# A recurrence and its MLP on one core: instruction order from a table instead of from priorities

## The chip, the cores and the metric

The kernel runs on one core of a Trainium2 chip. TensorE (PE) multiplies matrices, VectorE (DVE) and ScalarE (ACT) work element by element and move results out of PSUM, GpSimd (POOL) and SyncE (SP) mostly issue DMAs. Each engine runs its own instruction list in order, and the engines wait for one another through semaphores. The metric is the device time of one launch in microseconds; lower is better.

## What is computed

A recurrent layer with a matrix state for each of 4 x 8 heads runs over 768 positions, and its output goes through an MLP with the activation h tanh(softplus(h)).

```python
# B, H, S, D = 4, 8, 768, 40
state = zeros(B, H, D, D)
for t in range(S):
    y[:, :, t] = einsum('bhd,bhde->bhe', r_t, state)
    Sa = einsum('bhde,bhe->bhd', state, a_t)
    state = state * w_t[:, :, None, :] - einsum('bhd,bhe->bhde', Sa, b_t)
    state = state + einsum('bhd,bhe->bhde', v_t, k_t)
x = y.transpose(0, 2, 1, 3).reshape(B * S, H * D)     # 3072 x 320
h = x @ w_in                                          # 320 x 2048
g = h * tanh(softplus(h))
out = g @ w_out                                       # 2048 x 320
```

## The kernel before

**The recurrence in chunks.** The 768 positions are cut into 12 chunks of 64. Within a chunk the recurrence is solved with matrices, so that only one small state is passed from chunk to chunk. The work falls into preparation, which doesn't depend on the state, and steps, which do. Two chunks share one inverse; call them a pair. The letters are those that the change uses for units of work; c is a chunk, be one of two halves of its preparation, g one of two groups of heads in a step, n a pair.

- Preparation (`pre_a`, lines 126-203), for each (c, be): loads of decay and vectors (l), two scans and their products on VectorE (p, lines 145-170), a store of the decay products P to the DRAM tensor pD (line 172), the decay matrix (r, lines 162-168), eight Gram matmuls (g, lines 182-194) and transposes (k, lines 196-203).
- Inverse (`pre_inv`, lines 205-221), for each pair: i, a triangular inverse on VectorE, 60 dependent small instructions between transposes.
- After it (`post_inv`, lines 223-260): m, a corner product in two halves of 32 matmuls, with a copy by ScalarE between them (line 235); copies of blocks into bdT (b, d, lines 249-251); and a merge into KT (t, lines 255-260).
- A step (`step`, line 349), for each (c, g): the state is copied into VS (V, line 277); A multiplies it with KT (line 284), and ScalarE writes UVT (line 286); T transposes UVT (line 293); D transposes the state (line 304); B multiplies and VectorE masks (lines 314-316); C gives output and state change (lines 334-339), and VectorE builds the new state (lines 342-346). Then the output is stored to DRAM (yD), and v, u and q, the loads of the next chunk, are issued by GpSimd.

**The MLP.** x is the product of yD and pD, read back from DRAM (`load_yp`, lines 467-476) and split into two parts, xh and xl, so that products of reduced precision add up to full precision. Six blocks i of 512 rows are worked through, each in eight slices q: `mlp1` (h, line 584) makes 16 matmuls of 512 columns, ScalarE applies the activation (line 586), and the result is split (H, lines 589-590); `mlp2` (y, lines 604-606) makes 24 matmuls of 320 columns into four PSUM tiles. y runs three slices behind h. The weights come as 64-bit values and are converted and split on ScalarE and VectorE (`load_f32`, lines 445-464, and `split`, line 489): twelve conversions for w_in, eight for w_out.

**What sets the order.** The kernel is written in a program order, and a planner orders the instructions of each engine by priority and its own estimate of readiness. `at(tc, k)` (line 44) moves a part up or down by an offset from the table OFF (line 38), and ORDER and SORD set the order of the parts. The result is one fixed list for each engine; in the run nothing is reordered.

**Where the weights and the MLP stand.** The conversions of the first quarter of w_in (`early`) have priority over the start, the rest (`first`) stand with step 9, three of w_out (`second`) before step 10, and five (`third`) after the first slice of the MLP. The MLP itself is written behind the last step; its first blocks move forward among the last steps only as far as the planner moves them.

Of the kernel before, what the change touches and what calls it, by code (L numbers as in the profile page):

```python
# [36 lines left out]

OFF = {'I': 80, 'T1': 80, 'P00': -40, 'P10': 80, 'P11': 40, 'b0': 15, 'c0': 600, 'u0': -15, 'u1': 250, 'd0': 250,
       'd1': 150, 'W': 600, 'V': 400, 'E': 150, 'I0': 600, 'I1': 300, 'I2': 300, 'I3': 300, 'I4': 300, 'p4': 15,
       'I5': 300, 'J5': 600, 's0': 150, 's2': -15, 's3': 80, 's4': 250, 's6': -15, 's7': -40, 's8': 150, 's10': -150}  # L40
# [3 lines left out]
def at(tc, k):  # L44
    return tc.high_priority(offset=OFF[k]) if OFF.get(k) else nullcontext()

# [32 lines left out]
def attention(ctx, tc, I, yD, pD, nch, M):  # L79
    nc = tc.nc  # L80
# [3 lines left out]
    ps_u = pool("ps_u", NU, space=PSUM)  # L84
    ps_q = pool("ps_q", NQ, space=PSUM)
    ps_a = pool("ps_a", NA, ictx, "right", space=PSUM)
    M.early_pools(pctx)
    ps_g = pool("ps_g", NG, pctx, "right", space=PSUM)
# [18 lines left out]
    V.memset(z, 0.0)  # L107
    for w, b in zip(wab, bkb):
        V.memset(w, 1.0)
        G.memset(b, 0.0)  # L110
    for t in [d1] + [x.rearrange("p s k a t -> p (s k a t)") for x in adb[:NAD]]:
        A.copy(t, z.broadcast_to(t.shape))
    for t in bdT:
        G.memset(t, 0.0)
# [5 lines left out]
    for t in VS + [UVT] + bdr[:NBR] + ST:  # L120
        G.memset(t, 0.0)

    RW, W2, HA, BKN, GP, KT = {}, {}, {}, {}, {}, {}
    LQ, SQ, OQ, PQ = (dict(S=SP, G=G, A=A)[x] for x in QS)

    def pre_a(c, be):
        n = 2 * c + be
        wa, bk, ad = wab[n % NWA], bkb[n % NWA], adb[n % 2]
# [6 lines left out]
        if (c, be) == (0, 0):  # L135
            LQ.dma_start(out=cst, in_=I['cst'])
            for t in bkb:
                A.copy(t[:, :, 128:168], cst[:, 256:296].unsqueeze(1).broadcast_to([128, 8, 40]))
        wz, a = wa[:, 0:521], wa[:, 528:1040]
# [20 lines left out]
        if be == 1:  # L160

            RW[c] = wk.tile([128, 2, 16], F32, name="rw", bufs=4)
            pt = ps_g.tile([128, 2, 16], F32, name="pa")
            for b2 in range(2):
                for al in range(2):
                    PE.matmul(pt[b2 * 64:b2 * 64 + 64, al], ident[:, al * 64:al * 64 + 64], W2[b2].rearrange("p a b -> p (a b)"),
                              start=(al == 0), stop=True, skip_group_check=True)
            A.copy(RW[c], pt)
        bk4 = bk[:, :, 0:128].rearrange("p s (x t) -> p s x t", x=2)
        V.tensor_tensor(out=bk4, in0=bk4, in1=E3[:, :, 0:64].unsqueeze(2).broadcast_to([128, 8, 2, 64]), op=ALU.mult)  # L170
        for al in range(2):
            PQ.dma_start(out=pD[c, be, :, al], in_=P[al * 64:al * 64 + 40])

        if c % 2 == 0 and be == 0:
            GP[c // 2] = iw.tile([128, 32, 2, 32], F32, name="GP", bufs=NGP)
# [6 lines left out]
        for s0 in (0, 3, 6):  # L182
            m = min(3, 8 - s0)
            pt = ps_g.tile([128, 3, 168], F32, name="pa")
# [10 lines left out]

        bkn = wk.tile([128, 664], F32, name="bkn", bufs=NBKN)
        BKN[c, be] = bkn
        G.memset(bkn[:, 640:664], 0.0)
        for s0 in (0, 4):
            pt = ps_g.tile([128, 4, 2, 64], F32, name="pa")  # L200
# [4 lines left out]
    def pre_inv(n):  # L205
# [11 lines left out]
        TT = iw.tile([128, 32, 32], F32, name="TT", bufs=NTT)  # L217
        V.transpose(TT.rearrange("p u t -> p t u"), X)
        T1 = gp[0:64, :, 0]
        V.transpose(T1, TT[0:64])  # L220
        return TT, T1

    def post_inv(n, TT, T1):
        gp = GP[n]
        for h in range(2):
            with at(tc, 'T%d' % h):
                px = ps_a.tile([64, 16, 32], F32, name="pa")
                for j in range(16):
                    u = h * 16 + j
                    for al in range(2):  # L230
                        q = slice(64 + al * 32, 96 + al * 32)
                        PE.matmul(px[al * 32:al * 32 + 32, j], gp[q, u, 0], TT[q, u], start=(j == 0), stop=True,
                                  skip_group_check=True)
                X = iw.tile([64, 16, 32], F32, name="X2", bufs=NX2)
                A.copy(X, px)
                py = ps_a.tile([64, 16, 32], F32, name="pa")
                for j in range(16):
                    u = h * 16 + j
                    for al in range(2):
                        q = slice(al * 32, 32 + al * 32)  # L240
                        PE.matmul(py[q, j], T1[q, u], X[q, j], start=(j == 0), stop=True, skip_group_check=True)
                for be in range(2):
                    c = 2 * n + h
                    bd = bdT[be]
                    us = slice(h * 16 + be * 8, h * 16 + be * 8 + 8)
                    for al in range(2):
                        q0 = slice(al * 32, al * 32 + 32)
                        q1 = slice(64 + al * 32, 96 + al * 32)
                        A.copy(bd[q0, :, al, 0:32], TT[q0, us])  # L249
                        A.copy(bd[q1, :, al, 32:64], TT[q1, us])  # L250
                        A.copy(bd[q0, :, al, 32:64], py[q0, be * 8:be * 8 + 8])  # L251
# [407 lines left out]
```

## Time and profile before

| | us |
|---|---|
| median of 3 runs | 830.3 |
| lowest and highest run | 823.98 and 833.24 |
| span of the profiled execution, first to last instruction | 821.8 |
| TensorE busy in that span | 722.7 |
| VectorE busy | 458.7 |
| ScalarE busy | 428.7 |

The profile gives the span of the profiled execution; a time of its own beside that isn't shown, so 830.3 is set against 821.8, and 8.5 us lie between the median and the span. In a row of stages stand, after the limits and the length, the busy time and the count of instructions of TensorE's matmuls (PE), its weight loads (PEld), VectorE, ScalarE and GpSimd, then the granted TensorE clock as a share of full speed, the busy share of the DMA engines and GB/s. In a row of groups stand line, engine, operation, tiles written and read, shapes and count, then the busy time in us and the mean of one in ns, then the engine's idle time just before and what ended it. In a row of waits stand the waiting engine and line, what it waited for, the sum in us, the count, and the longest. A row of the chain has start, length and what ran. An fp32 matmul that isn't a transpose has two records in the trace; the table of the change counts it once.

### The profile page before, as it was taken

To read this page: it belongs to the slowest core of one execution; us is meant where nothing else is said; L and a number is where in the kernel's file an instruction comes from. 1 tells how busy PE (TensorE), PEld (TensorE's weight loads), DVE (VectorE), ACT (ScalarE), POOL (GpSimd) and SP (SyncE) were. 2 spreads that over 40 slices of the span, in tenths; PEclk is the share of its full clock that TensorE was granted. 3 is DMA by queue.
4 is the path that set the end of the run, shared out by engine and by line. 5 is a ranking of instruction groups with operands and counts; after the bars stand their busy time and mean duration, and the time that the engine had idled before them with its cause. 6 is when DMAs were issued, how large, how long until landed. Compare 5 with 4: busy or idle time off the path is not lost.

```text
span 821.8 us, 17217 instructions
## 1 busy us (share of the span) xinstructions
PE 722.7 (88%) x7048; PEld 644.8 (78%) x7048; DVE 458.7 (56%) x957; ACT 428.7 (52%) x931; POOL 103.4 (13%) x182
## 2 busy tenths in 40 slices
PE   2635798899889889888786899999999999999997
PEld 2524697788778778788676789999999999999997
DVE  6689878749899757988954558311312212111110
ACT  5533556784586867567685555343333333432331
POOL 8100012123223022221102100000000000000000
PEclk9855679999999999999999999999999999999999
DMA  6522224323433134423528755210300100000000
GB/s 169 143 65 81 57 53 96 99 67 97 118 103 76 59 96 105 83 58 111 142 76 207 160 157 135 59 51 1 77 33 0 55 17 1 33 1 1 33 1 32
DMA packets 58206, 61.81 MB, mean 75 GB/s; under 512 B 25536, under 2 KB 48704, under 8 KB 58128
## 3 DMA queue, kind: packets, MB, share of 16 engines
q1 hardware_dynamic: 49296, 40.94, 18.3%
q0 software_dynamic: 8832, 19.79, 10.0%
q8 instruction: 55, 0.90, 0.5%
q14 instruction: 23, 0.19, 0.1%
HBM read 48.79 MB, written 11.86 MB: 74 GB/s over the span
## 4 chain that ended last, share of the span: by engine, by line
PE 52%; ACT 9%; DVE 7%; DMA 3%; issue 2%; SPq 0%; ACTq 0%; DVEq 0%
PE ph L584 21%; PE po L605 7%; PE po L604 7%; PE po L606 7%; PE pa L258 2%; PE pa L186 2%; DMA xp<-pD 1%; DVE tmp L214 1%; DVE XL L216 1%; PE pq L314 1%; ACT bdT L249 1%; PE pu L284 1%; ACT bdT L250 1%; DMA cv_d<-in_wi 1%; ACT KT L260 1%
## 5 line engine op out<-in xcount | busy, mean ns | idle before, releaser
L590 DVE TENSOR_TENSOR gl<-g,gh 128x1024 fp32r<-128x1024 f32 x48 | 58.6, 1224 | 207.5 <-ACT gh L589 207.5
L586 ACT ACTIVATE g<-ph 128x512 f32<-128x512 f32 x96 | 57.3, 598 | 180.5 <-PE ph L584 180.3
L186 PE MATMUL pa<-bk,ad 128*128 128x168 f32 x384 | 85.6, 376 | 42.8 <-DVE bk L170 15.0
L604 PE MATMUL po<-w_oh,gh 128*128 128x320 f32 x384 | 118.3, 308 | 0.0
L605 PE MATMUL po<-w_ol,gh 128*128 128x320 f32 x384 | 118.3, 308 | 0.0
L606 PE MATMUL po<-w_oh,gl 128*128 128x320 f32 x384 | 118.3, 308 | 0.0
L584 PE MATMUL ph<-xh,w_ih 128*128 128x512 f32 x288 | 112.7, 393 | 2.0 <-ACT xh L568 2.0
L186 PEld LDWEIGHTS pa<-bk,ad 128*128 128x128 f32 x384 | 71.5, 235 | 48.2 <-issue 22.8
L584 PE MATMUL ph<-xh,w_il 128*128 128x512 f32 x288 | 97.1, 391 | 0.0
L584 PE MATMUL ph<-xl,w_ih 128*128 128x512 f32 x192 | 75.1, 391 | 0.0
L605 PEld LDWEIGHTS po<-w_ol,gh 128*128 128x128 f32 x384 | 72.1, 188 | 2.2
L604 PEld LDWEIGHTS po<-w_oh,gh 128*128 128x128 f32 x384 | 72.1, 188 | 1.8
L606 PEld LDWEIGHTS po<-w_oh,gl 128*128 128x128 f32 x384 | 72.1, 188 | 0.0
L584 PEld LDWEIGHTS ph<-xh,w_ih 128*128 128x128 f32 x288 | 54.1, 188 | 12.1 <-ACT xh L568 2.2
L584 PEld LDWEIGHTS ph<-xh,w_il 128*128 128x128 f32 x288 | 54.0, 188 | 11.6 <-issue 0.2
L216 DVE TENSOR_TENSOR XL<-XL,tmp 128x30 f32<-128x30 f32 (+9 forms) x180 | 58.7, 326 | 2.4
L214 DVE TENSOR_TENSOR tmp<-XL 128x30 f32<-128x30 f32 (+9 forms) x180 | 58.2, 324 | 2.3
L258 PE MATMUL pa<-bdT,HA 128*104 128x128 f32 x384 | 52.2, 289 | 7.0 <-ACT bdT L251 5.5
L258 PEld LDWEIGHTS pa<-bdT,HA 128*104 128x104 f32 x384 | 46.7, 179 | 11.1 <-ACT bdT L251 7.2
L314 PE MATMUL pq<-bdr,UVT 128*128 128x128 f32 x384 | 53.4, 284 | 0.4 <-ACT UVT L286 0.3
L334 PE MATMUL pq<-UVQ,bkn 128*64 128x104 f32 (+1 forms) x768 | 44.7, 254 | 7.8 <-DVE UVQ L316 5.5
L589 ACT CAST gh<-g 128x1024 fp32r<-128x1024 f32 x48 | 50.1, 1048 | 1.3
(89 smaller groups left out, 1212.6 us busy)
## 6 DMA issues: line engine op xcount, KB each, us to landing
wa<-in_wa SPq DMA_DIRECT2D x48, 162.5 KB
bk<-in_bk SPq DMA_DIRECT2D x48, 160.0 KB
cv_d<-in_wi SPq DMA_DIRECT2D x12, 512.0 KB
cv_d<-in_wo SPq DMA_DIRECT2D x8, 640.0 KB
pD<-P POOLq DMA_DIRECT2D x48, 81.2 KB, 2.2
VS<-in_vN POOLq DMA_DIRECT2D x24, 160.0 KB, 3.4
UVT<-in_vD POOLq DMA_DIRECT2D x24, 160.0 KB, 3.9
bdr<-in_rD POOLq DMA_DIRECT2D x24, 160.0 KB, 4.4
```

Source lines behind the costliest of these rows:

```text
L186: PE.matmul(pt[:, j], ad[:, s0 + j].rearrange("p k a t -> p (k a t)"), bk[:, s0 + j], start=(j == 0), stop=True, skip_group_check=True)
L214: V.tensor_tensor(out=tv, in0=X[:, i + 1:32, i:i + 1].broadcast_to([128, 31 - i, i]), in1=X[:, i:i + 1, 0:i].broadcast_to([128, 31 - i, i] ...
L216: V.tensor_tensor(out=X[:, i + 1:32, 0:i], in0=X[:, i + 1:32, 0:i], in1=tv, op=ALU.add)
L258: PE.matmul(pk[:, j], ha[:, s0 + j], bd[:, s0 + j].rearrange("p a t -> p (a t)"), start=(j == 0), stop=True, skip_group_check=True)
L314: PE.matmul(pq[:, s], UVT[:, g * 4 + s, be * 128:be * 128 + 128], br[:, be, g * 4 + s].rearrange("p a t -> p (a t)"), start=(s == 0), stop ...
L584: PE.matmul(ph, w, x, start=(n == 0), stop=(n == 7), skip_group_check=True)
L586: A.activation(g[:, j], ph, AF.Mish)
L589: A.copy(gh, g)
L590: V.tensor_tensor(out=gl, in0=g, in1=gh.bitcast(F32), op=ALU.subtract)
L604: PE.matmul(po[k], gh[:, j, t], oh, start=(f == 0), stop=False, skip_group_check=True)
L605: PE.matmul(po[k], gh[:, j, t], ol, start=False, stop=False, skip_group_check=True)
L606: PE.matmul(po[k], gl[:, j, t], oh, start=False, stop=(f == 15), skip_group_check=True)
```

## The change

Five things change; the arithmetic of the outputs stays.

1. The priorities go. Every part becomes a named unit (`U['A3.1']` is step A of chunk 3, group 1), `sequence()` writes the units in a program order, and `Lanes.order()` walks a table, PLAN, that lists for each of the five engines which unit's next instruction comes next. Consecutive instructions are joined by dependencies that carry order alone.
2. In the program order the load and split of x0, the last quarter of w_in (w3) and the first four slices h0.0 to h0.3 stand ahead of step 10, so ahead of the last two steps. In PLAN h0.0 follows D11.1.
3. Of w_in's first quarter only the loads and one conversion up to its last VectorE instruction stay at the start. The rest, and w1, w2 and w3, follow the inverse i5. All of w_out is converted in the MLP, in halves of 320 columns, with two load buffers (`CVA = 2`), in place, without the tile cv_m.
4. PSUM is four pools of two banks for the whole kernel; the h tiles alternate between those of Gram and inverse, the y tiles take those of the steps. g has two buffers for three; gh and gl keep six.
5. pD is stored in runs of 64 elements without the gap of one, and x is loaded with 12 DMAs for a block in place of 16, the decay in runs of 256 elements where it had 64.

```diff
-def at(tc, k):
-    return tc.high_priority(offset=OFF[k]) if OFF.get(k) else nullcontext()
+class Lanes:
+    def order(self):
+        queues = {}
+        for i in self.tc.nc.cur_bb.bb.instructions:
+            if self.of.get(i.name, '/')[0] not in '/+':
+                queues.setdefault(str(i.engine).split('.')[-1], {}).setdefault(self.of[i.name], []).append(i)
+        info = mybir.DependencyInfo(mybir.DependencyClass.NoSync, mybir.DependencyReason.DATA)
+        for e, plan in PLAN.items():
+            last, q = None, {k: iter(v) for k, v in queues[e].items()}
+            for t in plan.split():
+                k, n = (t.split('*') + ['1'])[:2]
+                for _ in range(int(n)):
+                    i = next(q[k])
+                    if last is not None:
+                        self.tc.add_manual_dep(i, last.name, info, reason='plan')
+                    last = i
+            assert all(next(x, None) is None for x in q.values())
...
+    for n in range(nds):
+        if n == nds - 1:
+            s.extend(('/i', '+i', 'x0', 'X0', 'w3'))
+            s.extend('%s0.%d' % (k, q) for q in range(NEA) for k in ('hH' if q < NGA else 'h'))
+        step(2 * n)
+        if n + 2 < nds:
+            pre(n + 2)
+        if n + 1 < nds:
+            inv(n + 1)
+        if n + 2 == nds:
+            s.extend(('/p', '+p', 'w0', 'w1', 'w2'))
+        step(2 * n + 1)
...
-            PQ.dma_start(out=pD[c, be, :, al], in_=P[al * 64:al * 64 + 40])
+            PQ.dma_start(out=pD[c, be, :, al].rearrange("e (s t) -> e s t", t=64), in_=P3[al * 64:al * 64 + 40, :, 0:64])
...
-                ph = ps_h.tile([128, T], F32, name="ph")
+                ph = (ps_g, ps_a)[nph[0] % 2].tile([128, T], F32, name="pa")
+                nph[0] += 1
...
+                for x, d in ((y, yD), (p, pD)):
+                    src = d[2 * i + c].rearrange("b e a (g t) -> (b e a g) t", g=2)
+                    SP.dma_start(out=x[:, 0:2, t], in_=src[0:256].rearrange("(k p) t -> p k t", k=2))
+                    for k in range(2):
+                        SP.dma_start(out=x[k * 64:k * 64 + 64, 2, t], in_=src[256:320])
```

Parts of PLAN, for TensorE the first merge and step, pair 1, and the end of the steps; for VectorE the start and steps 9 to 11; for SyncE the start and the MLP's first loads. `m1.0*32` means the next 32 matmuls of unit m1.0.

```
PE:  g3.1*6 m0.0*32 g3.1*2 k3.1*4 m0.0*32 k3.1*4 t0.0*4 g4.0*3 t0.0*4 g4.0*3 t0.1*8 A0.0*16 A0.1*16
...
     m1.0*32 r5*4 g5.1*3 m1.0*32 g5.1*5 t2.0*4 k5.1*4 t2.0*4 t2.1*4 k5.1*4 t2.1*4 m1.1*32
     A2.0*16 m1.1*32 A2.1*16 t3.0*4 B2.0*4 T2.0*8 B2.0*4 T2.1*8
...
     m2.0*32 r7*4 g7.1*3 m2.0*32 g7.1*5 t4.0*4
...
     A6.0*16 A6.1*16 T6.0*4 m3.1*32 B6.0*8 t7.0*4 g10.0*3 B6.1*8 T6.0*4 T6.1*4 t7.0*4 T6.1*4 D6.0*4 g10.0*5 C6.0*12 D6.1*4
...
     g11.1*6 m4.0*32 g11.1*2 m4.0*32 k11.1*4 t8.0*8 t8.1*8 m4.1*32 A8.0*16 m4.1*32 B8.0*8
...
     m5.1*32 A10.0*16 m5.1*32 A10.1*16 t11.0*8 T10.0*8 t11.1*4 T10.1*4 t11.1*4 B10.0*8 T10.1*4 D10.0*4
     B10.1*8 D10.1*4 C10.0*24 C10.1*24 A11.0*16 A11.1*16 D11.0*4 D11.1*4 h0.0*8 h0.1*8 h0.2*8 h0.0*8
     B11.0*8 h0.3*8 B11.1*8 h0.1*8 C11.0*24 h0.2*8 C11.1*24 h0.4*8 h0.3*8 h0.5*8 h0.4*8 h0.5*8 h0.6*8
     h0.7*8 h0.6*8 h0.7*8 h1.0*8 y0.0*12
DVE: z*3 w0*3 p0.0*6 p0.1 p0.0 p0.1 p0.0 p0.1*4 g0.0 p0.1 g0.0 p0.1 g0.0*2 g0.1 p1.0*6 g0.1*2 p1.1 g0.1 p1.0
...
     i5*7 C9.0 C9.1 w0*4 B9.0*2 B9.1 w0*2 B9.1 w0 C9.0 w0 C9.0*2 w0 C10.0 w1*3 C9.1*3 C10.1 w1*6 B10.0 w1
     B10.0 w1 B10.1*2 w1 w2 C10.0 w2*2 C10.0*2 w2 C10.1*3 X0*3 w2*8 B11.0*2 H0.0 B11.1 w3 B11.1 w3*3 H0.1
SP:  w0*2 l0.0*2 l0.1*2 l0.0*3 l0.1*2 w0 l1.0*2
...
     w1*3 w2 x0*12 w2*2 x1*4 w3 x1*7 w3 x1 w3 W0*2
```

More of the change, by code (lines that the diff above doesn't have):

```diff
@@ new lines, in blocks, with lower @@
+    def blocks(c, be):
+        n, bd = c // 2, bdT[be]
+        us = slice(c % 2 * 16 + be * 8, c % 2 * 16 + be * 8 + 8)
+        for al in range(2):
+            q0 = slice(al * 32, al * 32 + 32)
+            q1 = slice(64 + al * 32, 96 + al * 32)
+            A.copy(bd[q0, :, al, 0:32], TT[n][q0, us])
+            A.copy(bd[q1, :, al, 32:64], TT[n][q1, us])
+    def lower(c, be):
+        for al in range(2):
+            q0 = slice(al * 32, al * 32 + 32)
+            A.copy(bdT[be][q0, :, al, 32:64], PY[c // 2, c % 2][q0, be * 8:be * 8 + 8])
@@ new lines, in merge @@
+    def merge(c, be):
+        kt = wk.tile([104, 8, 128], F32, name="KT", bufs=NKT)
+        KT[c, be] = kt
+        ha = HA[c, be]
+        for s0 in (0, 4):
+            pk = ps_a.tile([128, 512], F32, name="pa")[0:104].rearrange("p (s t) -> p s t", s=4)
+            for j in range(4):
+                PE.matmul(pk[:, j], ha[:, s0 + j], bdT[be][:, s0 + j].rearrange("p a t -> p (a t)"), start=(j == 0), stop=True,
+                          skip_group_check=True)
+            A.copy(kt[:, s0:s0 + 4], pk)
@@ L414, with store @@
[L414 to L425 removed]
+    def store(c):
+        for be in range(2):
+            OQ.dma_start(out=yD[c, be], in_=YEV[c][be * 64:be * 64 + 40].rearrange("p a s t -> p a (s t)"))
+    for c in range(nch):
+        for be in range(2):
+            for k, f in dict(l=ld, p=scan, g=gram, k=natural, b=blocks, d=lower, t=merge).items():
+                U['%s%d.%d' % (k, c, be)] = partial(f, c, be)
+        U['r%d' % c] = partial(decay, c)
+        for g in range(2):
+            for k, f in dict(V=state, A=step_a, B=step_b, T=step_u, D=step_d, C=step_c).items():
+                U['%s%d.%d' % (k, c, g)] = partial(f, c, g)
+        for k, f in dict(v=load_vs, u=load_uv, q=load_r, o=store).items():
+            U['%s%d' % (k, c)] = partial(f, c)
@@ L426 @@
+    for n in range(nch // 2):
+        U['i%d' % n] = partial(inverse, n)
+        for h in range(2):
+            U['m%d.%d' % (n, h)] = partial(corner, n, h)
+    U['/p'] = pctx.close
+    U['/i'] = ictx.close
+I32 = mybir.dt.int32
+NQ1 = 3
+NEA = 4
+CVA = 2
 NX = 2
 NXP = 1
-NHB = 3
-NGB = 6
+NHB = 2
+NGA = 2
+NGB = 4
+NOS = 2
 LAG = 3
@@ L545, in third, with w_in @@
-    def third(self):
-        wp = self.pool("w2c", 1)
-        with self.tc.tile_pool(name="cvc", bufs=CVC, side="right") as cv:
-            self.w_out(wp, cv, range(NO1, 8))
-    def run(self, nsc):
+    def w_in(self, wp, cv, q):
+        h = wp.tile([128, 3, 512], F32R, name=f"w_ih{q}")
+        l = wp.tile([128, 3, 512], F32R, name=f"w_il{q}")
+        self.ih[q], self.il[q] = h, l
+        for k in range(3):
+            self.split(cv, h[:, k], l[:, k], self.I['wi'][:, (q * 3 + k) * 512:(q * 3 + k) * 512 + 512])
@@ L615, in run @@
+        U['+p'], U['+i'], U['+e'] = first, second, third
+        for q in range(4):
+            U['w%d' % q] = partial(w_in, q)
+        for q in range(8):
+            U['W%d' % q] = partial(w_out, q)
         for i in range(nsc // 2):
+            U['x%d' % i] = partial(load_x, i)
+            U['X%d' % i] = partial(split_x, i)
             for q in range(8):
-                wait.append((i, q) + mlp1(q, *x))
-                if (i, q) == (0, 0):
-                    self.third()
-                if q == 3 and i + 1 < nsc // 2:
-                    nx = load_x(i + 1)
```

589 lines of the change are left out of this document (323 added, 266 removed).

## The prediction, made before the changed kernel ran

> **What bounds the kernel now.** I read the page's span first, then busy time by stage, then the waits of TensorE, then those of VectorE at the start. The stages are cut where the chain changes: the first state matmul (A0, line 284) starts at 109.8 us, step 10 at 434.8, and from 480 the MLP runs alone.
>
> ```profile
> span 821.8 us, 17217 instructions
> core 0: us, PE busy (x) PEld busy (x) DVE busy (x) ACT busy (x) POOL busy (x), PEclk, DMA share, GB/s
> 0.00:50.00 50.00, 24.48 (x111) 21.00 (x112) 34.49 (x68) 25.48 (x65) 19.54 (x36) 0.86 0.53 141
> 50.00:100.00 50.00, 26.70 (x142) 22.07 (x142) 46.39 (x117) 19.75 (x58) 5.07 (x10) 0.62 0.24 70
> 100.00:109.80 9.80, 9.02 (x134) 8.23 (x128) 9.55 (x25) 6.24 (x15) 1.02 (x2) 0.50 0.35 86
> 109.80:434.80 325.00, 289.10 (x4337) 256.02 (x4338) 255.40 (x632) 226.61 (x574) 68.50 (x120) 0.98 0.34 90
> 434.80:480.00 45.20, 36.51 (x455) 30.72 (x452) 26.11 (x39) 23.60 (x43) 8.52 (x13) 0.96 0.79 168
> 480.00:816.00 336.00, 336.00 (x1883) 306.11 (x1882) 86.80 (x80) 125.73 (x176) 0.75 (x2) 1.00 0.14 39
> ```
>
> From 480 to 816 TensorE is never idle: no order can shorten that part unless work is taken out, and none is. Before it TensorE idles 49 us in the first 100, 325.0 - 289.1 = 35.9 us in the middle and 45.2 - 36.5 = 8.7 us in steps 10 and 11. In the start VectorE is the bound: 46.4 of 50 us busy between 50 and 100, and its inverse i0 must end before m0.0 can start. All that a new order can win lies in these stages.
>
> **The change part by part, by stage.**
>
> *Start (to A0.0).* The old order puts three whole conversions of w_in (lines 461-463, 495) into VectorE's first 50 us; the table keeps three instructions of one (w0*3) and sends the rest behind i5.
>
> ```profile
> L463 DVE SCALAR_TENSOR_TENSOR cv_w<-cv_d,cv_w 128x512 int32<-128x512 int32 x3 | 2.1, 691 | 0.1
> L462 DVE SCALAR_TENSOR_TENSOR cv_w<-cv_m,cv_w 128x512 int32<-128x512 int32 x3 | 2.1, 689 | 0.1
> L495 DVE SCALAR_TENSOR_TENSOR w_il<-cv_w,w_ih 128x512 fp32r<-128x512 f32 x3 | 2.0, 677 | 0.0
> L461 DVE TENSOR_SCALAR cv_w<-cv_m 128x512 int32<-128x512 int32 x3 | 1.3, 439 | 3.0 <-ACT cv_m L459 2.8
> 7.15 0.69 DVE L463 SCALAR_TENSOR_TENSOR cv_w<-cv_d,cv_w 128x512 int32<-128x512 int32 x1
> DVE HA L191 <- ACT HA L190: 6.6, 7, 2.2
> DVE wa L157 <- ACT ad L155: 3.8, 3, 1.6
> DVE GP L193 <- ACT GP L189: 0.4, 1, 0.4
> cv_d<-in_wi SPq DMA_DIRECT2D x12, 512.0 KB
> ```
>
> The three cost 2.1 + 2.1 + 2.0 + 1.3 = 7.5 us; what stays is 0.44 + 0.69 + 0.69 = 1.8; so 5.7 us leave VectorE ahead of i0. The waits of VectorE between 7.5 and 50 us sum to 10.8. The table puts instructions of the next scan into them (p0.1 between the last ones of p0.0, p1.1 between those of p1.0), where the old order mostly stands still. Between 0 and 10.8 I take half, 5.4, since the filler itself waits for loads. Against it: SyncE now issues two 512 KB loads of w_in ahead of l0.0's data, where there was one: 0.52 MB at the 141 GB/s of that stage is 3.7 us, or nothing if the loads were not what VectorE waited for (it is busy with the first conversion until 7.8). I take 2.0. Start: -5.7 - 5.4 + 2.0 = -9.1 us, between -16.5 and -2.0.
>
> *Middle (A0.0 to step 10).* The same matmuls in another order; the dependencies that hold it join instructions of one engine and add none. The largest waits of TensorE, and the rows that price them:
>
> ```profile
> PE pa L258 <- ACT bdT L251: 5.5, 5, 1.5
> PE pu L293 <- ACT UVT L286: 4.9, 5, 1.9
> PE pa L241 <- ACT X L235: 4.5, 5, 2.1
> L286 ACT ACTIVATE UVT<-pu 128x512 f32<-128x512 f32 x24 | 14.4, 600 | 15.3 <-PE pu L284 15.2
> L235 ACT COPY X<-pa 64x512 f32<-64x512 f32 x12 | 6.9, 573 | 0.3 <-PE pa L232 0.2
> L251 ACT COPY bdT<-pa 32x256 f32<-32x256 f32 x48 | 17.3, 361 | 3.8 <-PE pa L241 3.0
> 312.65 1.91 PE pa L186 x12
> 247.41 0.69 PE pu L284 x16
> ```
>
> Each of the three is a round trip over ScalarE: a corner product to its copy to the merge (m, d, t), a state product to its copy to the transposes (A, T), the two halves of m. In the table nearly all of them have other matmuls between the two ends. m1.0 and t2.0 are parted by five of g5.1, which are ten records of 1.91 / 12 = 0.16 us, so 1.6 us over two copies of 0.36. A6.0 and T6.0 are parted by A6.1, 32 records or 1.4 us over a copy of 0.60. The halves of m2.0 are parted by r7 and three of g7.1. The thin ones are four of twelve halves of m, with a bare A.0 between (m1.1, m4.1, m5.1) or two of g11.1 (m4.0). I take three quarters of 14.9 us: 11.2. The other 21.0 us are many small waits on evacuations; in-order queues that drift from the table's durations will make new ones, so I take a quarter: 5.3. Middle: -16.5 us; the ends are -35.9 (no idle left) and 0 (every wait only changes place).
>
> *Steps 10 and 11.*
>
> ```profile
> PE pu L293 <- ACT UVT L286: 3.3, 2, 2.6
> PE pq L334 <- DVE UVQ L316: 3.1, 1, 3.1
> PE ph L584 <- ACT xh L568: 2.0, 1, 2.0
> 451.31 0.49 DVE L461 TENSOR_SCALAR cv_w<-cv_m 128x640 int32<-128x640 int32 x1 [3.47 <-ACT cv_m L459]
> 451.72 0.68 DVE L316 TENSOR_TENSOR UVQ<-pq,cst 128x512 f32<-128x512 f32 x1
> 452.46 0.76 PE L334 MATMUL pq<-UVQ,bkn 128*64 128x104 f32 x12 [3.15 <-DVE UVQ L316]
> ACT cv_m L459 <- DMA cv_d<-in_wo: 5.6, 1, 5.6
> ```
>
> The wait on UVT is covered: m5.1 and t11.0 now stand between A10 and T10, so 3.3 us go. x0's twelve loads fetch the decay in runs of 256 elements instead of 64, in twelve DMAs where sixteen were, and h0.0 stands after A11 and D11, not ahead of A11.1: of the 2.0 us on xh I take 1.0. The 3.1 us stay: conversions w1 and w2 stand ahead of step masks as before. The h blocks between D11 and B11 win nothing by themselves; they are the same matmuls drawn forward. -4.3 us, between -8.7 and 0.
>
> *MLP.* Each h and y pair takes a fixed time:
>
> ```profile
> 490.72 3.65 PE ph L584 x16
> 799.18 3.65 PE ph L584 x16
> L495 DVE SCALAR_TENSOR_TENSOR w_ol<-cv_w,w_oh 128x640 fp32r<-128x640 f32 x8 | 6.6, 823 | 4.8 <-ACT w_oh L494 4.7
> L172 POOL DMA_DIRECT2D pD<-P x48 | 25.0, 525 | 186.2 <-DVE w L150 72.8 <-DVE tmp L214 42.8 <-DVE P L147 40.6
> L270 POOL DMA_DIRECT2D UVT<-in_vD x24 | 18.1, 757 | 57.1 <-PE pq L314 57.1
> ```
>
> 43 steps in 308.46 us, 7.17 each. All eight w_out tiles are converted here, in halves, where three were done earlier. An instruction on a half lies between half of 823 ns and the 690 of a 512-wide one; 16 halves of four are 26 to 44 us on a VectorE that has 336 - 86.8 = 249 us free. Cost 0; the cover is lost only if W0 is late for y0.0, which ten half blocks of h (ten of 1.83 us) precede. Buffers of g (2 for 3) and gh/gl (still 6) are freed by y and split_g blocks ahead: 0. The stores of pD become runs of 64 elements: a POOL issue between 525 ns and the 757 of UVT, at most 11 us on an engine with over 250 us free in the middle: 0. The reordered loads v, u, q keep their place behind the reads that free their tiles: 0.
>
> **Sum.** -9.1 - 16.5 - 4.3 = -29.9 us: span 791.9. The median of 830.3 lies 8.5 over the profiled span, so 800.4, rounded to 800.
>
> **The rivals.**
>
> *Everything is covered.* If three quarters of every idle stage goes and the start reaches -11, it is -11 - 26.9 - 6.5 = -44.4: 786. For it speaks that all three large waits have one remedy; against it that VectorE is itself busy 255 of 325 us.
>
> ```profile
> PE pa L186 <- DVE bk L170: 15.0, 1, 15.0
> PE pa L186 <- ACT ad L155: 10.6, 1, 10.6
> PE pa L186 <- DVE HA L191: 6.8, 2, 6.3
> ```
>
> *The clock.* The granted clock is 0.62 and 0.50 in the two rows to 109.8, after waits of 15.0, 10.6 and 6.3 us, and 0.98 in the middle, where no wait is over 2.1. At full clock the 9.02 us before A0.0 would take 4.5, another -4.5: 796. The table fills VectorE's waits, not TensorE's during i0, so I don't add it; 1 in 20, inside the case above. The Trainium skill says the same ("TensorE: Matmul & The Clock Gate", Part 1): half clock after an idle window of some 3.4 us, full after as long a busy one. By that rule, as the trace agrees, the start stays slow and the sum stands.
>
> *VectorE becomes the bound.* If masks and scans stand behind inverse instructions that are drawn forward, about half of the gain is left: -15, 815.
>
> *The waits only change place.* The old order is also a fixed one, and interleaves too. Then middle and end give nothing and the start some 4: 826.
>
> *Conversions block the steps: slower.* VectorE is in order. In the rows above one conversion waits for its load and the mask of B10 behind it makes TensorE wait 3.15 us. The table has nine whole conversions (w1, w2, w3) from step 9 on, with two load buffers, and x0's and x1's loads stand in the same SyncE queue. At the 5.6 us that ScalarE waited there, nine cost 50.4, net +20.5: 851. It cancels the gain at 29.9 / 9 = 3.3 us each and is slower by over 1% from 4.2.
>
> **How the numbers follow.** One per cent, 8.3 us, is about what this measurement tells from no change. Forecast 0.50; all covered 0.12; VectorE bound 0.13; waits change place 0.13; conversions block 0.12. Faster is the first three, 0.75; same 0.13; slower 0.12. The range reaches from 784, just under the covered case, to 832, past the case of no change; the slower case is left out, with some 0.05 below. The forecast's own range is 788 to 813.
>
> **What would show it.** Right: A0.0 starts near 100 us; step 10's A near 409; the waits on bdT, UVT and X sum to under 5 us; MLP steps stay at 7.17 without idle TensorE. Wrong: VectorE conversions with idle time before them from cv_m and masks queued behind; new TensorE waits on evacuations in the middle; an idle TensorE before y0.0.

## The result, and the profile after

The new kernel takes 757.2 us (median of 4 runs, 754.1 to 760.3) where the kernel before took 828.2 beside it: ratio 0.914, 95% interval 0.908 to 0.920. A second series gave 757.7 us and 0.919 (0.915 to 0.923). So the direction was right and the size was not: 71 us were won where 30 were forecast, and 757 lies far under the range's low end of 784.

The page of the new kernel, and its busy time by stage (columns as before: the stretch, its length, then busy time of each engine, granted clock, DMA share, GB/s). The stages are cut at the same events, the first state matmul A0 at 105.5, step 10's at 367.0 and the end of the last step at 417.8:

```profile
span 754.3 us, 17264 instructions
```

```profile
0.00:50.00 50.00, 21.60 (x112) 17.34 (x112) 36.12 (x71) 24.19 (x63) 22.32 (x38) 0.91 0.58 151
50.00:100.00 50.00, 27.36 (x249) 23.32 (x250) 46.55 (x106) 22.84 (x67) 5.66 (x8) 0.67 0.23 64
100.00:105.50 5.50, 5.50 (x39) 5.36 (x37) 4.85 (x19) 3.36 (x8) 0.00 (x0) 0.79 0.36 88
105.50:367.00 261.50, 254.78 (x4221) 235.00 (x4220) 243.80 (x617) 211.72 (x550) 75.82 (x123) 1.00 0.41 100
367.00:417.80 50.80, 45.60 (x572) 40.41 (x568) 30.73 (x47) 32.35 (x62) 7.55 (x12) 0.93 0.58 165
417.80:749.00 331.20, 331.20 (x1869) 302.35 (x1866) 104.63 (x132) 127.04 (x199) 1.00 (x2) 1.00 0.15 47
```

| stage | before | after | change | forecast |
|---|---|---|---|---|
| start to A0.0 | 109.8 | 105.5 | -4.3 | -9.1 |
| middle, A0.0 to A10.0 | 325.0 | 261.5 | -63.5 | -16.5 (0 to -35.9) |
| A10.0 to the end of the span | 387.0 | 387.3 | +0.3 | -4.3 |
| span | 821.8 | 754.3 | -67.5 | -29.9 |

The middle is nearly everything. It fell by more than the whole idle time that it held, 35.9 us, which the forecast had called its bound. TensorE's busy time there fell too, from 289.1 to 254.8, though the matmuls are nearly the same ones. The last stage kept its length although half of m5.1 and the merges t11 moved into it, 4.7 us of TensorE's work at the pace used below.

The waits of TensorE in the middle answer the forecast's first test; here is the new kernel's list (in all, times, longest):

```profile
PE pa L411 <- ACT bdT L402: 1.2, 1, 1.2
PE pa L353 <- DVE HA L340: 1.0, 3, 0.4
PE pq L466 <- ACT yev L498: 0.9, 1, 0.9
PE pa L388 <- issue: 0.8, 2, 0.4
PE pa L388 <- ACT X L382: 0.7, 2, 0.4
PE pa L411 <- ACT KT L413: 0.5, 2, 0.3
PE pu L449 <- ACT UVT L443: 0.2, 1, 0.2
```

The waits on bdT, UVT and X, 14.9 us in 15 waits before, are 2.1 us in four. What the waits' list can't show stands in the groups of the two kernels: the 640 state products of ten steps (line 284 before, 441 after) in the middle, columns count, busy time, mean ns of one, idle time before them; first the kernel before:

```profile
L284 PE MATMUL pu<-KT,VS 104*64 104x64 f32 x640 | 31.9, 230 | 0.9 <-ACT smd L305 0.6 <-ACT KT L260 0.2
```

and the new one:

```profile
L441 PE MATMUL pu<-KT,VS 104*64 104x64 f32 x640 | 22.4, 224 | 0.1
```

The same instructions on the same shapes are busy 31.9 us in one and 22.4 in the other, at 0.9 and 0.1 us of idle before them; the mean length of a record hardly moved (230 and 224 ns). Records overlap, so busy time is set by how closely one starts behind another. A group's busy time exaggerates the difference, for each run of records has an end that lies over the next group's, and the 640 stand in 52 runs before and in 16 after. Counted from each record's start to the start of TensorE's next, without idle time, they take 28.8 and 21.3 us. What stretches them stands in the timeline of the kernel before (start, length, records):

```profile
113.27 0.33 PE L284 MATMUL pu<-KT,VS 104*64 104x64 f32 x2
113.53 0.24 PE L232 MATMUL pa<-TT,GP 32*32 32x32 f32 x2
113.70 0.33 PE L284 MATMUL pu<-KT,VS 104*64 104x64 f32 x2
113.96 0.24 PE L232 MATMUL pa<-TT,GP 32*32 32x32 f32 x2
```

The planner put state products (A) and corner products (m) one by one between each other. Such a round of four records takes 0.43 us, from 113.27 to 113.70; at the pace of unbroken runs it would be 0.09. Busy TensorE is not a fixed amount of work. The Trainium skill ("Perfetto Trace Analysis", Identifying the Most-Contended Engine) calls matmul busy time no good measure of how close a kernel is to its limit, because pipelined instructions look smaller in the trace; a middle whose busy time fell by 34.3 us, only 7.4 of it moved work, agrees.

To see what filled the busy time, each step from one record's start to the next was set against the pace that its kind keeps in the new kernel when it follows its own kind at full clock (state product 0.030 us, corner product 0.016, merge 0.114, gram 0.152 and so on). A kind is a letter of the units (g, r, k, m, t, A, T, D, B, C). Worked out from all records of the middle and the granted clock:

```
us in the middle                                before   after   change
work at that pace                                243.5   236.1     -7.4   (moved: 4.7 behind A10.0, 2.7 ahead of A0.0)
TensorE idle                                      35.9     6.7    -29.2
steps at half clock, beyond the pace               5.0     0.0     -5.0   (10.2 and 0 us at half clock)
last record before an idle stretch, in full       12.2     4.4     -7.8   (70 and 25 of them)
steps to another kind                             18.3    12.3     -6.0   (259 and 224; of all changes 323 and 242)
other, most of it just behind a change            10.2     2.1     -8.1
sum                                              325.0   261.5    -63.5
```

So 29 us of the 63 are idle time, 7 are work that moved out of the stage, and the rest was hidden in busy time: 14 at changes of kind and just behind them, 8 in last records, 5 at half clock. That is a way of sorting records, not yet a proof of causes; for that come the experiments.

### The profile page after: what moved, and what is told of

It reads as the page before. It is cut to its first block, busy times and chain, and to the rows that moved or that the text cites. A ratio compares the mean times of both kernels' runs of the same rounds, so it can differ in the third digit from the quotient of the medians.

```text
span 754.3 us, 17264 instructions
## 1 busy us (share of the span) xinstructions
PE 686.4 (91%) x7048; PEld 623.9 (83%) x7048; DVE 466.7 (62%) x989; ACT 422.3 (56%) x947; POOL 112.4 (15%) x182
## 4 chain that ended last, share of the span: by engine, by line
PE 63%; ACT 13%; DVE 12%; DMA 5%; issue 4%; SPq 0%; DVEq 0%; ACTq 0%
PE pa L662 24%; PE pu L686 4%; PE pu L684 4%; PE pq L686 4%; PE pu L685 4%; PE pq L684 4%; PE pq L685 4%; PE pq L466 3%; PE pa L335 3%; PE pa L411 3%; DVE tmp L365 2%; DVE XL L367 2%; DMA wa<-in_wa 2%; ACT bdT L397 2%; PE pu L449 2%
## 5 line engine op out<-in xcount | busy, mean ns | idle before, releaser
L662 PE MATMUL pa<-xh,w_ih 128*128 128x512 f32 x288 | 113.7, 395 | 0.0
L662 PE MATMUL pa<-xh,w_il 128*128 128x512 f32 x288 | 97.5, 393 | 0.0
L662 PE MATMUL pa<-xl,w_ih 128*128 128x512 f32 x192 | 75.5, 393 | 0.0
L662 PEld LDWEIGHTS pa<-xh,w_il 128*128 128x128 f32 x288 | 54.5, 189 | 11.6
L686 PE MATMUL pq<-w_oh,gl 128*128 128x320 f32 x192 | 59.4, 309 | 0.0
L686 PE MATMUL pu<-w_oh,gl 128*128 128x320 f32 x192 | 59.4, 309 | 0.0
L684 PE MATMUL pu<-w_oh,gh 128*128 128x320 f32 x192 | 59.3, 309 | 0.0
L684 PE MATMUL pq<-w_oh,gh 128*128 128x320 f32 x192 | 59.2, 309 | 0.0
L685 PE MATMUL pq<-w_ol,gh 128*128 128x320 f32 x192 | 59.2, 309 | 0.0
L685 PE MATMUL pu<-w_ol,gh 128*128 128x320 f32 x192 | 59.2, 308 | 0.0
```

What stands on the lines that cost most here:

```text
L662: PE.matmul(ph, w, x, start=(n == 0), stop=(n == 7), skip_group_check=True)
L684: PE.matmul(po[i][k], gh[:, j, t], oh, start=(f == 0), stop=False, skip_group_check=True)
L685: PE.matmul(po[i][k], gh[:, j, t], ol, start=False, stop=False, skip_group_check=True)
L686: PE.matmul(po[i][k], gl[:, j, t], oh, start=False, stop=(f == 15), skip_group_check=True)
```

## The experiments

All times below are medians against the new kernel's 757.2 and, in the second series, 757.7 us, unless another is named; ratios are to the kernel before, run beside each. The second series of the new kernel:

> The new kernel as it stands, for the comparison with the next runs on the same chip: 757 us, ratio 0.914 (0.908 to 0.920).

**Is it the order at all?** The change also rewrites helpers, halves loads and moves blocks of the program. In old_order every attention instruction is listed in the kernel before's order on each engine; the MLP's keep their places in the new table. The program's own loop over a step changes with it:

```
-        for k in 'VABTD':
+        for g in range(2):
+            for k in 'VABTD':
...
```

> The new kernel with everything it has (pools, in-place conversions moved behind i5, x loads, early h blocks), but with the instructions of the recurrence listed in the order that the kernel before had on each engine; only the MLP's instructions keep their places. Order theory (the order in the middle is what saved the time): most of the gain is gone, 805 to 830 us, middle from the first to the eleventh state product 310 to 325 us as before, with TensorE idle 25 us or more in it. Structure theory (moved conversions, pools and loads saved the time): 755 to 780 us, middle under 280 us.

Measured 831.2 us, ratio 1.000 (0.997 to 1.003), 1 us above what the order theory had said; the middle is 336.6 us long, 35.8 of them idle. In the old order everything else is worth nothing that can be measured, so the gain hangs on the order. Whether the new order would win as much without the pools and the moved conversions was not run. This profile also shows what the old order can lose to the clock: 37.5 us of its middle stand at half clock, 19.1 us lost, where the profile of the kernel before has 10.2 and 5.0.

**Which table?** no_table leaves all tables out (the call of order()), pe_only keeps TensorE's alone, no_pe keeps all but TensorE's. What a table doesn't hold, the planner orders.

```
no_table
-        M.ln.order()
pe_only
-        for e, plan in PLAN.items():
+        for e, plan in [('PE', PLAN['PE'])]:
no_pe
-        for e, plan in PLAN.items():
+        for e, plan in [x for x in PLAN.items() if x[0] != 'PE']:
```

> The new kernel without the order-only dependencies: the planner orders by program order, without table and without the old priorities. Order theory: slower than the kernel before, 840 to 950 us, since program order puts a whole pair's preparation and inverse between two steps. Structure theory: 760 to 800 us.

> The table for TensorE alone; the other four engines are ordered by the planner around it. If TensorE's order is what counts and the others follow from it: 757 to 775 us. If the orders of VectorE and ScalarE carry their own part: 780 to 830 us.

> The table for VectorE, ScalarE, GpSimd and SyncE, TensorE by the planner. If TensorE's order counts: 790 to 850 us. If it follows from the other four, which fix when its operands are ready: 757 to 780 us.

Measured: no_table 847.7 us, ratio 1.019 (1.013 to 1.025); pe_only 846.8, 1.019 (1.012 to 1.027); no_pe 821.4, 0.989 (0.983 to 0.995). Neither part brings the gain. Against no_table, the same program without any table, TensorE's table alone is worth 1 us, the other four without it 26, all five 90; against the kernel before, whose priorities no_table lacks, the four win 9 us of 71. pe_only lies above both of its forecasts. In the middle of pe_only TensorE stands idle for other engines' results that come in another order than its own:

```profile
PE pu L441 <- ACT VS L433: 5.9, 4, 3.6
PE pu L457 <- ACT UVQ L450: 5.9, 4, 3.0
PE pa L353 <- DVE HA L340: 4.7, 3, 3.9
PE pq L466 <- DVE UVQ L468: 4.6, 4, 2.8
```

An order on one engine moves a wait to where the next engine's order puts it. The expectation that one table carries most of the gain falls.

**What does one wait cost?** In halves the second half of each of the twelve corner products stands directly behind its first, so that TensorE must sit out ScalarE's copy between them; what stood between follows. The same for all twelve:

```
-  m1.0*32 r5*4 g5.1*3 m1.0*32 g5.1*5
+  m1.0*64 r5*4 g5.1*8
```

> The new kernel, with the second half of each of the 12 corner products (32 matmuls) directly behind its first half on TensorE; between the halves ScalarE copies the first's result, and with nothing in between TensorE must wait for that copy. All other tables are unchanged, and the matmuls that stood between the halves follow them. It puts 12 bare round trips back, 10 of them in the middle. Theory 'an uncovered wait costs its idle time' (0.9 us by the kernel before's waits on X): +9 to +12 us. Theory 'a wait costs more than its idle time, through the last matmul's full latency ahead of it and the lower clock behind it': +13 to +20 us, with half-speed records in the middle again. Rival 'another engine sets the middle and takes it up': 0 to +5 us.

Measured 788.7 us, ratio 0.953 (0.950 to 0.955), and 787.8 (0.956, 0.948 to 0.963) when run again: some 31 us, 2.6 for each wait. The idle time accounts for less than half. The middle of halves:

```profile
107.70:399.80 292.10, 271.29 (x4287) 252.51 (x4286) 243.71 (x616) 214.96 (x555) 77.40 (x126) 0.93 0.36 91
```

Its waits on the copy (in all, times, longest):

```profile
PE pa L387 <- ACT X L381: 13.7, 11, 1.5
```

It is 30.6 us longer than the new kernel's 261.5; TensorE's idle time went from 6.7 to 20.8 (+14.1), its busy time from 254.8 to 271.3 (+16.5) for the same work, and the granted clock from 1.00 to 0.93. One of the twelve places, in order of time (start, length, records; the wait in brackets), and then the busy time and clock of the window ahead of the state products and of the one with them:

```profile
161.46 1.20 PE L378 MATMUL pa<-TT,GP 32*32 32x32 f32 x64
164.18 1.20 PE L387 MATMUL pa<-X,GP 32*32 32x32 f32 x64 [1.52 <-ACT X L381]
165.31 3.56 PE L440 MATMUL pu<-KT,VS 104*64 104x64 f32 x64
169.07 2.04 PE L410 MATMUL pa<-bdT,HA 128*104 128x128 f32 x8 [0.20 <-ACT bdT L401]
```

```profile
162.69:166.10 3.41, 1.92 (x85) 1.80 (x85) 3.27 (x10) 2.19 (x5) 0.00 (x0) 1.00 0.30 84
166.10:172.93 6.83, 6.54 (x64) 6.29 (x62) 3.95 (x9) 4.65 (x11) 3.80 (x6) 0.50 0.42 110
```

A single wait of 1.52 us leaves TensorE busy 1.92 of 3.41 us; the next 6.83 us run at half clock, where 64 state products take 3.56 us and eight merges 2.04. In all 39.1 us of the middle stand at half clock. Sorted as above, it holds 17.4 us of half-clock loss, the new kernel's none, and the last records before idle stretches 5.0 against 4.4. So the theory "a wait costs more than its idle time" was right, by the clock and not by the last records, and even its 13 to 20 us was too low.

**Is it the clock, or what the wait shifts?** halves_warm and halves_warm6 fill the same places with matmuls that nobody needs, written into the second half's buffer ahead of its own products, twelve of them in halves_warm and six in halves_warm6. The copy comes no sooner.

```
         py = PY[n, h] = ps_a.tile([128, 512], F32, name="pa")[0:64].rearrange("p (j t) -> p j t", j=16)
+        for j in range(12):
+            PE.matmul(py.rearrange("p j t -> p (j t)")[:, 0:128], ident[:, 0:64], ident, start=True, stop=True, skip_group_check=True)
```

> The kernel of halves (788.7 us; the second half of each corner product directly behind its first), with 12 matmuls of 64 columns of weights by 128 that nobody needs between the halves, written into the second half's buffer ahead of its own products: some 1.4 us at each of the 12 places, where halves stood idle 1.2 us. They need nothing of the copy, which comes no sooner. Theory 'most of the price of a wait is the half clock that follows it': no half-speed stretch in the middle, and of halves' 31 us over the new kernel only the filled waits are left, 12 times 1.4 us and little else: 770 to 778 us. Rival 'the price is the wait itself and what it shifts': 786 to 792 us, as halves.

> As halves_warm, with 6 useless matmuls at each of the 12 places; they are 12 records of 0.11 us, 1.4 us a place, as 12 were 24 records and 2.76 us. Theory 'the half clock is what a wait costs beyond its idle time': no half-speed stretch in the middle, and 12 x 1.4 us less than halves_warm: 774 to 780 us, 9 to 15 us faster than halves although TensorE does 0.8 us x 12 of work more. Rival 'the price is the wait itself and what it shifts': 786 to 792 us, as halves.

> The kernel of halves once more, beside halves_warm6 on the same chip: 788 to 790 us, ratio 0.950 to 0.955, with about eight half-speed stretches in the middle.

halves_warm took 792.6 us, as the rival said, but for a dull reason: each of the twelve is two records, so a fill lasted 2.76 us, twice the wait. It had one half-clock window of 3.4 us in the middle, where halves has 39.1 us of them. With half as many, halves_warm6 took 778.1 us, ratio 0.944 (0.937 to 0.950), beside 787.8 of halves on the same chip: TensorE does 12 x 1.46 = 17 us of useless work more and the kernel is 10 us shorter. The same place and the whole middle in halves_warm6 (line 384 is the filler):

```profile
159.66 1.20 PE L378 MATMUL pa<-TT,GP 32*32 32x32 f32 x64
160.92 1.52 PE L384 MATMUL pa<-cst 128*64 128x128 f32 x12
162.38 1.20 PE L389 MATMUL pa<-X,GP 32*32 32x32 f32 x64
163.51 2.09 PE L442 MATMUL pu<-KT,VS 104*64 104x64 f32 x64
166.57 1.12 PE L412 MATMUL pa<-bdT,HA 128*104 128x128 f32 x8 [0.98 <-ACT bdT L403]
```

```profile
106.40:389.40 283.00, 272.62 (x4417) 251.56 (x4416) 245.16 (x622) 214.60 (x555) 76.91 (x124) 0.99 0.38 93
```

The second half starts 1.5 us behind the end of the first, as in halves, but the state products behind it take 2.09 us instead of 3.56. On the same chip halves_warm6 took 776.5 to 782.1 us and halves 782.6 to 790.2, so no run of the one reaches the other, though the intervals of their ratios overlap a little; and the records show the same: 17.4 and 13.7 us lost to half clock in the middle of halves' two profiles, 1.5 here. That the lower clock behind short waits is a large part of their price is shown.

**What do the moved MLP blocks do?** h_late puts the h blocks that stand among the last step's matmuls behind them, on three engines.

```
-  D11.1*4 h0.0*8 h0.1*8 h0.2*8 h0.0*8 B11.0*8 h0.3*8 B11.1*8 h0.1*8 C11.0*24 h0.2*8 C11.1*24
+  D11.1*4 B11.0*8 B11.1*8 C11.0*24 C11.1*24 h0.0*8 h0.1*8 h0.2*8 h0.0*8 h0.3*8 h0.1*8 h0.2*8
```

> The new kernel, with the 56 first-layer matmuls that stand between the attention's last matmuls (h0.0 to h0.3, some 13 us of TensorE by the MLP's 7.17 us for 16 of them and 24 of the second layer, by columns) put behind the last of C11.1, on TensorE, and with them on ScalarE and VectorE what belongs to them (Mish, the copy to the rounded form, the differences, the next block's X). Theory 'they fill round trips of the last step': the stretch from A10.0 to the first second-layer matmul keeps the same work and gains the idle time that they covered; the last step's own round trips bare were 8.7 us of idle in the last two steps of the kernel before, so +5 to +9 us, and the idle stands before D11, B11 and C11. Rival 'they only changed places': 0 to +2 us, with idle before B11 and C11 that comes back as less idle before y0.0.

Measured 765.3 us, 0.924 (0.921 to 0.928): +8 us, as the covering theory had it. The idle time that the blocks covered comes back mostly at one place, the wait on the step mask (h_late, from step 10's A on; the wait on UVT stands in the new kernel too, with 2.9 us):

```profile
PE pq L466 <- DVE UVQ L468: 5.0, 1, 5.0
PE pu L457 <- ACT UVT L443: 2.7, 1, 2.7
PE pa L662 <- ACT g L664: 1.9, 1, 1.9
```

VectorE reaches that mask late, because X0 and conversions of w_in stand ahead of it in its table (h_late):

```profile
397.86 0.69 DVE L568 SCALAR_TENSOR_TENSOR cv_w<-cv_d,cv_w 128x512 int32<-128x512 int32 x1
399.25 0.69 DVE L588 SCALAR_TENSOR_TENSOR w_il<-cv_w,w_ih 128x512 fp32r<-128x512 f32 x1 [0.70 <-ACT w_ih L587]
399.86 1.28 DVE L468 TENSOR_TENSOR UVQ<-pq,cst 128x512 f32<-128x512 f32 x2
```

**Does changing between kinds of matmul cost?** Sorted as above, a step to another kind takes 55 ns (new kernel) to 71 ns (kernel before) more than its pace. alternate makes 66 more changes, wherever a C c.1 and a k meet, as here:

```
-  C3.1*24 k7.0*8
+  C3.1*3 k7.0 C3.1*3 k7.0 C3.1*3 k7.0 C3.1*3 k7.0 C3.1*3 k7.0 C3.1*3 k7.0 C3.1*3 k7.0 C3.1*3 k7.0
```

> The new kernel, with 66 more changes between kinds of matmul on TensorE and no new wait: where a step's second output group C c.1 (24 matmuls) stands next to transposes of a later block (k, 4 or 8), they alternate, three or six to one. If a change between kinds costs the 55 to 66 ns that the records show at such places, +4 us (3.6 to 4.4). If it costs nothing by itself and the records show something else there (pipelining across different tiles), within 1 us of the new kernel.

Measured 771.6 us, 0.932 (0.929 to 0.936): +14 us, and both theories missed. One return trip in alternate:

```profile
181.41 0.71 PE L492 MATMUL pq<-UVQ,bkn 128*64 128x104 f32 x12
182.63 0.33 PE L356 MATMUL pa<-cst,bk 128*128 128x128 f32 x1 [0.51 <-DVE HA L343]
182.89 0.40 PE L492 MATMUL pq<-UVQ,bkn 128*64 128x104 f32 x4
```

A k drawn forward now waits for VectorE's HA (5.7 us in six waits in the middle, 1.0 in the new kernel), which the edit wasn't meant to do. Sorted as above, of the middle's 14.0 us 3.6 are idle time and 8.3 stand at 60 more changes of kind seen there, 140 ns each, twice the average of the old ones; the other 2.1 are spread. Changes cost, more between these two kinds than on average; why, no run here tells apart. The kernel before has 323 changes in its middle and the new one 242, and the last two terms of the table, at the changes and mostly just behind them, fell from 28.5 to 14.4 us: 14 us of the gain, by the sorting, though no run puts the old order's one-by-one mixture alone into the new one.

**Does VectorE hold the kernel now?** dve_extra adds 24 fills of a spare tile in the middle; old_extra the same on old_order; no_bk leaves the bk multiply out of 20 of 24 scans; bk_pool and bk_pool_all give it to GpSimd for 5 and for 20 scans; copy_act moves 24 copies of 128 x 8 to ScalarE.

```
dve_extra, old_extra
+            V.memset(spare, 0.0)
no_bk, bk_pool, bk_pool_all
-        V.tensor_tensor(out=bk4, in0=bk4,
+        if n < 4: V.tensor_tensor(out=bk4, in0=bk4,
+        (G if 4 <= n <= 8 else V).tensor_tensor(out=bk4, in0=bk4,
+        (G if n >= 4 else V).tensor_tensor(out=bk4, in0=bk4,
copy_act
-        V.tensor_copy(w2[:, 1], P[:, 64:520:65])
+        A.copy(w2[:, 1], P[:, 64:520:65])
-        V.reciprocal(d1[:, 64:584:65], w2[:, 1])
+        V.reciprocal(d1[:, 64:584:65], P[:, 64:520:65])
```

> The new kernel with 24 more VectorE instructions, fills of a spare tile of 128 x 512 that nobody reads, six in each of the runs of inverses i1 to i4, so all of them in the middle (A0.0 to A10.0). About 0.46 us each, 11 us in all by estimate. VectorE is busy 243.8 of the middle's 261.5 us in the new kernel, TensorE 254.8. Theory 'TensorE's own work sets the middle now': 0 to +3 us, VectorE's share of the middle goes to 97%. Rival 'VectorE and TensorE bound it together, the orders leave no slack between them': +6 to +12 us, with TensorE idle before m, T or the matmuls behind HA and UVQ.

> The kernel of old_order (before's order, 831.2 us) with the same 24 fills of a spare tile on VectorE, six in each of i1 to i4 at the same places of their instructions; they took 0.36 us each in dve_extra, 8.6 us in all. In the new kernel they cost 5.2 us. If VectorE was not the bound in the old order (busy some 255 of its middle's 336 us), 0 to +3 us; if the masks and inverses behind them were already on the path there, +5 to +9 us.

> The new kernel without the last multiply of the scans from p2.0 on (bk by E stays undone in 20 of 24 scans, 1.22 us each on VectorE, 5 of them ahead of A0.0). Theory 'VectorE bounds the start and shares in bounding the middle': A0.0 4 to 6 us earlier; the middle no further than its busy TensorE, -2 to -6 us; 745 to 752 us. Rival 'TensorE's table alone sets the pace': 755 to 758 us.

> The new kernel, with the last multiply of the scans p2.0 to p4.0 (bk by E, 128 x 1024, 1.18 to 1.23 us each on VectorE) on GpSimd, ahead of that scan's two stores; five of VectorE's multiplies leave the stretch before A0.0, 6.1 us. Theory 'VectorE bounds the start': A0.0 comes 3 to 6 us earlier and the kernel is 3 to 6 us shorter. Rival 'GpSimd is slow at it (estimate 2 to 4 us each) and what waits for bk, or VectorE beside it, loses the time': 0, or slower by up to 6 us, with TensorE waiting on bk before g2 to g4.

> As bk_pool, for all scans from p2.0 on: 20 multiplies, 24 us, go from VectorE to GpSimd, 18 us of them in the middle by their places or just ahead of it. If VectorE bounds the middle together with TensorE as dve_extra showed (5.2 of 8.6 us came out), the middle shrinks, but no further than TensorE's 254.8 busy us: 0 to -6 us beyond bk_pool. Rival 'GpSimd's loads of v, u and q, which stand behind these multiplies in its order, come later, and the steps wait': +3 to +15 us beyond bk_pool.

> The new kernel, with the 24 copies of the scans' last decays (128 x 8, 0.17 us each where nothing stands beside them) on ScalarE instead of VectorE, and the second reciprocal reading the scan's result itself. VectorE loses 24 x 0.17 = 4 us, 1.5 of them ahead of A0.0, ScalarE gains as many. If VectorE holds the start and half of the middle, -1 to -3 us against the new kernel; if ScalarE's evacuations are as tight, 0 to +2 us.

dve_extra took 762.5 us, 0.921 (0.918 to 0.924): +5 us, for 8.6 us more of VectorE's busy time; the middle grew from 261.5 to 267.7. That lies between the two theories: VectorE is close behind TensorE. old_extra took 834.1 us, ratio 1.012 (1.007 to 1.018), against old_order's 831.2; its profiled span is shorter than old_order's (832.1 and 833.5), and its middle holds 6.1 us more idle time (41.9 and 35.8) but 7.6 less lost to half clock (11.5 and 19.1); so what the fills cost the old order stays open. no_bk took 751.2 us, 0.910 (0.904 to 0.917): 24 us of VectorE's work taken out win 6 at most, with A0.0 at 103.2 and the middle at 259.1, where TensorE is busy 253.7. VectorE is not what holds most of the time. copy_act's 755.9 us, 0.915 (0.910 to 0.919), can't be told from the new kernel, and no version that does all of the work clearly beats it.

bk_pool took 759.3 us, 0.921 (0.916 to 0.926), with A0.0 at 109.6, 4 us later instead of earlier, and bk_pool_all 791.8, 0.960 (0.955 to 0.965), with TensorE waiting 25.0 us on GpSimd's bk (18.2 of it at one place ahead of A0.0) and 12.1 on loads of r (bdr) queued behind these multiplies. The first multiply of bk_pool, on GpSimd:

```profile
62.15 2.18 POOL L307 TENSOR_TENSOR bk<-bk,wa 128x1024 f32<-128x1024 f32 x1 [27.00 <-DVE wa L303]
```

and VectorE beside it:

```profile
60.45 0.41 DVE L367 TENSOR_TENSOR XL<-XL,tmp 128x240 f32<-128x240 f32 x1
...
62.34 2.25 DVE L367 TENSOR_TENSOR XL<-XL,tmp 128x240 f32<-128x240 f32 x1
64.52 1.23 DVE L293 TENSOR_TENSOR_SCAN P<-wa,d 128x520 f32<-128x520 f32 x1
```

An addition of 0.41 us took 2.25 and ended 0.26 us behind GpSimd's multiply. Beside each of the five moved multiplies one such VectorE instruction lasts 1.78 to 2.40 us. Moving this one relieved VectorE of 1.2 us and blocked it for 1.8.

## Why the prediction was right in direction and wrong in size

*Middle.* The mechanism held: corner, merge, state and transpose products wait on round trips over ScalarE, and the table covers these. The step that failed is the sentence "the ends are -35.9 (no idle left) and 0": it priced the same matmuls with TensorE's busy time fixed at 289.1 us, so that idle time was all there was to win. The middle won 63.5 us: 29.2 of idle, 7.4 of work moved, and 27 that had stood as busy. By the sorted records these 27 are 14.1 at changes of kind and just behind them, 7.8 in last records before idle stretches, shown in full, and 5.0 at half clock. Two of these prices the experiments put into the new kernel: in alternate changes between kinds cost, 140 ns each by the records, and in halves a wait costs 2.6 us for 1.2 of idle, the rest by the half clock. How the 27 us divide between them is the sorting of records alone, and the clock's part differs between profiles of the same order of the recurrence: 5.0 us in this one, 19.1 in old_order's.

The shares taken were too small as well. Three quarters of the three large waits and a quarter of the rest made 16.5; 29.2 of 35.9 went, as the small waits on evacuations (21.0 before) went with the large. No new waits came from queues that drift, since the other engines' tables agree with TensorE's; no_pe and pe_only show how it goes when they don't.

*The clock.* The rival gave it 4.5 us, in the start only, since the middle's mean clock was 0.98. A mean of 0.98 over 325 us still holds 10.2 us at half clock, three stretches of 3.4, which lost 5.0 us. The rule cited there, half clock after an idle window of some 3.4 us, doesn't hold in that form here: in halves, under half a window was enough (below).

*Start.* -9.1 against -4.3. The conversions' term came: they take 7.5 us of VectorE ahead of A0.0 before and 1.9 after. The filler's 5.4 us hardly came: VectorE's idle time there went from 19.4 to 18.0. Its largest wait is the same as before, behind ScalarE's evacuations of the gram products, 7.9 us in eight; here is the first instruction of i0 in the new kernel:

```profile
46.34 2.09 DVE L360 STREAM_TRANSPOSE XL<-GP 128x1024 f32<-128x1024 f32 x1
```

The inverse i0 begins at 46.3 instead of 49.9 and m0.0 at 91.7 instead of 99.3. So up to m0.0 7.6 of the 9.1 us were won. But m0.0 to A0.0, which the forecast had left as it was, takes 13.8 us where it took 10.5, with more of t, g and k in between, 2.7 us of it work that the middle had done before. A0.0 was forecast near 100 and came at 105.5. That the start is VectorE's only in part shows in no_bk: 6.1 us less ahead of A0.0 bring it 1.6 to 2.3 us forward.

*Steps 10 and 11, and the MLP.* The stage from A10.0 kept its length while 4.7 us of work moved into it, so some 4.4 us were won against 4.3 forecast. That the size fits is in part luck, for other waits went than those named. The 3.3 us on UVT in step 10 went, but one of 2.9 came at D11.1, where ScalarE casts x0 first:

```profile
392.93 1.47 ACT L645 CAST xh<-xy 128x1536 fp32r<-128x1536 f32 x1 [1.55 <-DVE xy L644]
394.30 0.59 ACT L443 ACTIVATE UVT<-pu 128x512 f32<-128x512 f32 x1
394.95 0.66 PE L457 MATMUL pu<-cst,ST 128*128 128x128 f32 x4 [2.86 <-ACT UVT L443]
```

In its place the wait on the mask, which the prediction had left standing at 3.1, and all of the 2.0 on xh went. "The h blocks between D11 and B11 win nothing by themselves" was wrong: h_late loses 8 us without them, 5.0 of it the wait on the mask. The MLP came out at 0 as forecast: from 417.8 TensorE is never idle, and h and y are busy 347 us in all against 346.

*The rivals.* That waits only change place falls. That VectorE becomes the bound is half right, and late: it costs a few us at 757, not 40. Conversions do stand ahead of a step's mask, as the slower rival had it, but at one place and for 5.0 us, and the new kernel hides that behind the h blocks; nine at 5.6 us each didn't come. "Everything is covered", 786, had the mechanism that came nearest, and it too counted idle time alone.

## What to carry to other kernels

Don't take TensorE's busy time as fixed when an order changes. Compare the steps from start to start of equal matmuls between two orders, count how often the kind changes, and look at the granted clock window by window, not at its mean. In this kernel a bare wait of over a microsecond, repeated twelve times, cost about twice its idle time, so matmuls that fill it are worth having even if they do nothing useful, as long as they don't outlast it: six to a place won 10 us, twelve won nothing. And an order helped only where every engine in the round trip kept one that agrees.

## What the runs showed of the hardware

**Half clock after a wait, not only after an idle window.** From 150 us on in halves, nine half-clock stretches follow 3.4 us windows in which TensorE was idle for 0.29 to 0.67 of the time, five of them at 0.40 to 0.44, as in the rows above (1.92 of 3.41 us busy). In the new kernel a window with 0.36 idle stayed at full clock behind it, so no sharp bound shows:

```profile
317.30:320.71 3.41, 2.18 (x29) 1.69 (x23) 3.23 (x7) 3.23 (x9) 0.00 (x0) 1.00 0.02 5
320.71:324.10 3.39, 3.05 (x31) 2.61 (x32) 3.01 (x12) 3.24 (x8) 0.00 (x0) 1.00 0.00 0
```

In the kernel before some windows at 0.5 kept the full clock and one half-clock stretch, at 116.5, follows a window without idle time, so the share of idle time isn't the whole rule. The Trainium skill ("TensorE: Matmul & The Clock Gate", Part 1) has the same window of 3.4 us, and its table of states puts the half clock after at least one idle window; if that means a window idle throughout, the trace disagrees.

**A two-input instruction of VectorE stands still beside GpSimd's multiply.** The 0.41 us addition that took 2.25 us beside GpSimd's multiply agrees with the Trainium skill ("SBUF — State Buffer", Who interferes with whom): an instruction of VectorE with two inputs in SBUF and one of GpSimd that reads SBUF take a shared port in turn, each for its whole length. The four other multiplies of bk_pool show the same, with 1.78 to 2.40 us. A scan (1.23 us) directly behind the first had its usual length.
